# Attention's products with v taken chunk by chunk, and the last 64 keys turned by transpositions

## The chip, the cores and the metric

The kernel runs on one core of a Trainium2 chip. The metric is the device time of one execution in microseconds (us). Engines are named as in the profile: PE is TensorE's matmul queue and PEld its weight loads, DVE is VectorE, ACT is ScalarE, POOL is GpSimd, SP issues most of the transfers.

## The reference

Two parts follow each other: attention over batch 4, 8 heads, 576 positions, head width 64, with a bias that a small network makes of the distance between positions, and a gated feed-forward layer over the 2304 tokens.

```python
scores = q @ k.T / 8 + bias[head]          # 576 x 576 per batch and head
attn = exp(scores - max); attn /= sum(attn)
x = (attn @ v)                              # tokens x 512
h = x @ w_in                                # 512 -> 2048
out = (h * tanh(softplus(h))) @ w_out       # 2048 -> 512
```

The change lies in attention alone, in how `attn @ v` and the transpositions ahead of it are cut up.

## The kernel before, in words

Attention goes over 16 pairs `i`: a pair is one batch and two heads, head 0 in partitions 0 to 63 (`TOP`), head 1 in 64 to 127 (`LOW`). The 576 query rows of a pair are cut into chunks: 0 to 3 with 128 rows, 4 with 64. A step `n` is one chunk of one pair; the chunks of a pair come in the order 0, 1, 4, 2, 3, so 80 steps in all (`x = n % 5`, `c` the chunk). Below, "step x=2" is the third step of a pair.

For its own chunk a step does: `scores(n)` on PE (L226: two heads at once in two halves of the array, three passes of 2 x 288 keys; the first three pairs are in plain float32), `add_bias(n)` on DVE (L243: two instructions, one per head, that take the scores out of PSUM, add the bias and find the row maximum), and `exps(n)` on ACT (L258). The scores have two PSUM buffers per step's two heads in such a way that the scores of a step can begin only when `add_bias` of the step before has emptied them.

A product with v needs the weights with keys on partitions. `transposes(n)` turns chunk n's rows for keys 0 to 511 of both heads by 16 PE transpositions (L296), into two PSUM banks, which ACT copies to the tile `main` (L305, two copies of 128 x 512). The last 64 keys of both heads lie side by side in 128 columns of `pt`; `ends(n)` turns them by two ordinary float32 matmuls against the identity (L321), each of which PE runs as two passes, into a third bank, and ACT copies the result into `tail` (L322). Chunk 4 has its end among the transpositions.

`pv_duo(i, grp, k)` is the product with v: group 0 is chunks 0 and 1 (256 query columns, one `main0`), group 1 is chunks 4, 2, 3 (320 columns). For each of five key blocks k it does one matmul per head (L335, for the last block L339), again two passes each; the two heads stand in two column halves of the array and run side by side. After the fifth block DVE copies the result out of PSUM (L342) and SP stores it to `x_d`. The `products` table in `step` spreads these blocks: two at x=4, two at x=0, one at x=1, three at x=2, two at x=3.

The order on every engine is the order of the calls in `step(n)` (the schedule is manual): scores and bias of n, transpositions of chunk n-2, exponentials of n, reciprocals of the pair before (at x=0), loads ahead, one piece of the conversion of float64 weights (`split`, mostly DVE, L125 to L132; on ACT at x=2), products, and at x=1 and x=4 an extra `ends`. Steps 0 to 2 run inside the stage that makes the bias; steps 3 and 4 have an order of their own. Four more steps, NS to NS+3, finish the last chunks among the first units of the feed-forward layer (`hidden`, L623).

Of the kernel before, what the change touches and what calls it, by code (L numbers as in the profile page):

```python
# [7 lines left out]
F32 = mybir.dt.float32  # L8
# [7 lines left out]
B, H, S, D, C = 4, 8, 576, 64, 32  # L16
# [3 lines left out]
P = 128  # L20
# [25 lines left out]
def kernel(ctx: ExitStack, tc, qk, v, wb, w2, w_in, w_out, psia, psi4, rinv, eye, out):  # L46
# [225 lines left out]
    def turned(i, grp):  # L272
        if (i, grp) not in pt_t:
            w = 256 if grp == 0 else 320
            main = ptp.tile([P, 2, 4, w], F32, name=f"main{grp}")
            tail = ptp.tile([P, 256 if grp == 0 else 384], F32, name=f"tail{grp}")[:, :w]
            pt_t[i, grp] = (main, tail)
        return pt_t[i, grp]

    def place(c):  # L280
        return (0, c * P) if c < 2 else (1, 64 + (c - 2) * P)

    def transposes(n, shared=False):
        i, c = steps[n]
        pt, m = live[n]
        main, tail = turned(i, 0 if c < 2 else 1)
        top, low = (t_ps.tile([P, 512], F32, name="tp") for _ in range(2))
# [9 lines left out]
        inline = c in (2, 3) or (c < 2 and i == 0)  # L297
        if inline:
            copy_end = ends(n)
        if c < 4:  # L300
            off = place(c)[1]
            for g, tp in enumerate((top, low)):
                q0 = off + 64 * g
                copy = dve.tensor_copy if shared and g else act.copy
                copy(main[:, :, :, q0:q0 + 64], tp.rearrange("p (h k q) -> p h k q", h=2, k=4))  # L305
            if inline:
                copy_end()
        else:
            for h, tp in enumerate((top, low)):
                act.copy(main[:, h, :, 0:64], tp[:, :256].rearrange("p (k q) -> p k q", k=4))  # L310
                act.copy(tail[(TOP, LOW)[h], 0:64], tp[(LOW, TOP)[h], 256:320])

    def ends(n):

        i, c = steps[n]
        pt, m = live[n]
        grp, off = place(c)
        tail = turned(i, grp)[1]
        end = t_ps.tile([P, 512], F32, name="tp")
        for h in range(2):  # L320
            pe.matmul(end[h * 64:h * 64 + 64, 0:P], pt[:, 512 + 64 * h:576 + 64 * h], ident, start=True, stop=True)  # L321
        return lambda: act.copy(tail[:, off:off + P], end[:, 0:P])  # L322

    def pv_duo(i, grp, k):
        hp, b = divmod(i, B)
        main, tail = pt_t[i, grp]
        vt = v_t[i]
        w = 256 if grp == 0 else 320
        if k == 0:
            o_t[0] = o_ps.tile([P, 512], F32, name="o")  # L330
        o = o_t[0]
        kw = dict(skip_group_check=True)
        if k < 4:
            for h in range(2):
                pe.matmul(o[h * 64:h * 64 + 64, :w], vt[:, h, k, :], main[:, h, k, :],  # L335
                          start=(k == 0), stop=False, **kw)
            return
        for h in range(2):
            pe.matmul(o[h * 64:h * 64 + 64, :w], vt[:, h, 4, :], tail, start=False, stop=True, **kw)  # L339
        del pt_t[i, grp]  # L340
        x = xs.tile([P, 320], F32, name="x")
        dve.tensor_copy(x[:, :w], o[:, :w])  # L342
        if grp == 0:
            sp.dma_start(out=x_d[b][:, hp, 0:256], in_=x[:, :256])
        else:
# [67 lines left out]
    def step(n):  # L413
        i, x = divmod(n, 5)

        def begin():
            if n < NS:
                scores(n)
                add_bias(n)

        def turn():
            if 0 <= n - LAG < NS:
                transposes(n - LAG)
            if x == 4 and i:
                ends(n - 3)()

        def end():
            if 0 <= n - 1 < NS and (n - 1) % 5 == 4:
                reciprocals((n - 1) // 5)
            if n < NS:  # L430
                ahead(n)
                split(n)

        def products():
            todo = {4: (i, 0, (0, 1)), 0: (i - 1, 0, (2, 3) if i < NPAIR else (2, 3, 4)), 1: (i - 1, 0, (4,) if i < NPAIR else ()), 2: (i - 1, 1, (0, 1, 2)),
                    3: (i - 1, 1, (3, 4))}.get(x, (-1, 0, ()))
            j, grp, ks = todo
            if 0 <= j < NPAIR and (j, grp) != (0, 0):
                for k in ks:
                    pv_duo(j, grp, k)  # L440

        if n in (3, 4):
            scores(n)
            if n == 3:
                transposes(0, True)
            add_bias(n)
            exps(n, 0)
            if n == 3:
                transposes(1, True)
            exps(n, 1)  # L450
            if n == 3:
                transposes(2)
            else:
                for k in range(5):
                    pv_duo(0, 0, k)
            end()
            return
        begin()
        turn()
        if n < NS:  # L460
            exps(n, 0)
            exps(n, 1)
        end()
        products()
        if x == 1 and n < NS:
            ends(n - 1)()
# [105 lines left out]
    ptp = lsbuf("ptp", 1)  # L572
# [5 lines left out]
    t_ps = lpsum("t_ps", 3)  # L578
# [72 lines left out]
    step(NS + 3)  # L651
# [247 lines left out]
```

## Time and profile before

| | us |
|---|---|
| median of 3 runs | 667.78 (667.48 to 668.13) |
| the profiled execution's own time | 669.82 |
| its span, from the first to the last instruction | 667.8 |
| mean granted TensorE clock over the span | 0.994 |

PE is busy for 96% of the span, PEld for 75%, DVE for 68%, ACT for 62%, POOL for 23%. These are means over stages with different limits: the stage that makes the bias reaches to about 60 us, attention to about 296 us, the feed-forward layer to the end. A busy PE in the profile is not PE at its peak, since the ends of matmuls are modelled and overlap; how often PE starts a pass says more than how long it counts as busy.

### The profile page before, as it was taken

The page shows a single profiled execution, that of the slowest core. Times are in us where ns is not written, and L with a number is a line of the kernel's source. Part 1 is how long each engine was busy: PE and PEld are TensorE (multiplying, and loading weights), DVE is VectorE, ACT ScalarE, POOL GpSimd, SP SyncE. Part 2 cuts the span into 40 slices and gives each one's busy share as a digit, 9 for nine tenths or more (in the row PEclk, how much of TensorE's full clock was granted, in tenths as well). Part 3 has the DMA queues.
Part 4 walks back from the last instruction along what each step waited for, and adds up shares of the span by engine and source line. Part 5 has one row for each costly group of instructions (what it writes and reads, how often), then busy time and mean ns, then how long its engine had stood idle before and what let it go on. Part 6 is the DMA issues. An engine that isn't in the chain of part 4 may idle for free.

```text
span 667.8 us, 13803 instructions
## 1 busy us (share of the span) xinstructions
PE 644.1 (96%) x5300; PEld 499.4 (75%) x5300; DVE 450.8 (68%) x822; ACT 412.0 (62%) x871; POOL 150.7 (23%) x142
## 2 busy tenths in 40 slices
PE   6868999999999999999999999999999999999997
PEld 3214667777777777778888998888888888888886
DVE  7995777778888786721433455334699877888874
ACT  6995799989999889862433343343574444454441
POOL 0000133333222231701102120112243321133330
PEclk9997999999999999999999999999999999999999
DMA  4998486677667858106448786733764544433300
GB/s 134 307 313 266 146 253 208 219 224 241 217 219 229 263 167 258 44 19 194 152 153 258 253 220 194 217 124 122 225 190 126 158 151 149 142 117 117 114 32 33
DMA packets 101058, 119.66 MB, mean 179 GB/s; under 512 B 15616, under 2 KB 77568, under 8 KB 100992
## 3 DMA queue, kind: packets, MB, share of 16 engines
q1 hardware_dynamic: 98688, 110.59, 52.5%
q0 software_dynamic: 1872, 8.09, 3.9%
q8 instruction: 42, 0.69, 0.4%
q14 instruction: 24, 0.20, 0.1%
q10 hardware_dynamic: 432, 0.09, 0.1%
HBM read 79.47 MB, written 39.28 MB: 178 GB/s over the span
## 4 chain that ended last, share of the span: by engine, by line
PE 82%; DMA 4%; ACT 3%; DVE 2%; issue 2%; SPq 0%; POOL 0%; DVEq 0%; ACTq 0%
PE h L623 30%; PE s L226 10%; PE o L335 9%; PE y L745 8%; PE h L745 8%; PE tp L296 5%; PE y L746 4%; PE h L746 4%; PE tp L321 3%; PE o L339 2%; DMA x_d<-x 1%; ACT pt L258 1%; DMA xa<-r_d 1%; ACT main L305 1%; DMA xraw<-x_d 1%
## 5 line engine op out<-in xcount | busy, mean ns | idle before, releaser
L258 ACT ACTIVATE pt<-pt,m 128x576 f32<-128x576 f32 x144 | 112.3, 790 | 2.3 <-DVE m L243 2.3
L243 DVE CUSTOM_DVE_ANT_0 pt<-s,bias 128x576 f32<-128x576 f32 (+1 forms) x112 | 81.5, 754 | 34.0 <-PE s L226 31.8
L635 ACT ACTIVATE g<-h 128x512 f32<-128x512 f32 x72 | 42.8, 599 | 73.1 <-PE h L623 61.4
L305 ACT COPY main<-tp 128x512 f32<-128x512 f32 x126 | 68.1, 598 | 25.0 <-PE tp L296 23.5
L335 PE MATMUL o<-main,vt 128*64 128x320 f32 (+1 forms) x512 | 75.9, 420 | 0.0
L177 POOL TENSOR_TENSOR qklo<-rawqk,qkhi 128x304 fp32r<-128x304 f32 x52 | 43.7, 865 | 122.5 <-DMA rawqk<-in_qk_dram 122.5
L639 POOL TENSOR_TENSOR g<-g 128x256 f32<-128x256 f32 (+1 forms) x40 | 33.4, 837 | 159.5 <-ACT g L635 150.5
L623 PE MATMUL h<-xa,lc 128*128 128x512 f32 (+1 forms) x288 | 55.5, 354 | 0.0
L296 PEld LDWEIGHTS tp<-ident,pt 64*128 64x128 f32 x1184 | 51.2, 139 | 4.9 <-ACT main L305 2.4
L296 PE MATMUL tp<-ident,pt 64*128 64x64 f32 x1184 | 52.6, 223 | 2.0 <-ACT main L305 1.9
L623 PEld LDWEIGHTS h<-xa,lc 128*128 128x128 f32 x288 | 47.6, 189 | 7.5
L722 DVE TENSOR_TENSOR gslot<-quarters,gslot 128x1024 fp32r<-128x1024 f32 x28 | 47.0, 1704 | 7.9 <-ACT gslot L721 7.9
L721 ACT CAST gslot<-w 128x1024 fp32r<-128x1024 f32 x30 | 31.5, 1051 | 32.0 <-DVE w L718 19.0
L554 PE MATMUL bps<-ht,w2t 128*32 128x512 f32 (+17 forms) x352 | 35.3, 510 | 16.3 <-ACT bt L536 7.8
L722 DVE TENSOR_TENSOR gslot<-w,gslot 128x1024 fp32r<-128x1024 f32 x30 | 41.1, 1384 | 13.6 <-ACT gslot L721 13.6
L226 PE MATMUL s<-qkhi 64*128 64x288 f32 x260 | 49.3, 343 | 0.1
L721 ACT CAST gslot<-quarters 128x1024 fp32r<-128x1024 f32 x28 | 29.5, 1052 | 31.3 <-DVE quarters L718 19.8
L226 PEld LDWEIGHTS s<-qkhi 64*128 64x128 f32 x260 | 28.1, 184 | 25.9 <-DVE m L243 11.4
L335 PEld LDWEIGHTS o<-main,vt 128*64 128x64 f32 x512 | 33.4, 139 | 17.0 <-issue 2.3
L524 DVE TENSOR_SCALAR ht<-at,bb 128x576 f32<-128x576 f32 (+17 forms) x123 | 44.1, 440 | 0.0
L226 PE MATMUL s<-qklo,qkhi 64*128 64x288 f32 x260 | 42.0, 296 | 0.1
L226 PE MATMUL s<-qkhi,qklo 64*128 64x288 f32 x260 | 41.2, 293 | 0.4 <-POOL qklo L177 0.4
(157 smaller groups left out, 1482.6 us busy)
## 6 DMA issues: line engine op xcount, KB each, us to landing
g_d<-g SPq DMA_DIRECT2D x32, 512.0 KB
bias_d<-bt SPq DMA_DIRECT2D x36, 295.5 KB
w<-in_w_in_dram SPq DMA_DIRECT2D x16, 512.0 KB
w<-in_w_out_dram SPq DMA_DIRECT2D x16, 512.0 KB
quarters<-g_d SPq DMA_DIRECT2D x16, 512.0 KB
qkhi<-in_qk_dram POOLq DMA_DIRECT2D x13, 608.0 KB, 4.9
rawqk<-in_qk_dram SPq DMA_DIRECT2D x13, 608.0 KB
w<-g_d SPq DMA_DIRECT2D x15, 512.0 KB
```

What stands on the lines that cost most here:

```text
L226: pe.matmul(s[:, j, :SH], q[rows, c * P:(c + 1) * P], k[rows, KO + j * SH:KO + (j + 1) * SH], start=(t == 0), stop=(t == len(terms) - 1))
L243: dve.tensor_tensor_reduce(out=halves(pt[rows, sl]), in0=s[rows, :, :SH], in1=halves(bt[rows, sl]), scale=-0.125, scalar=BIG, op0=ALU.add, ...
L258: act.activation(ps, ps, AF.Exp, bias=m[:, u:u + 1], scale=-1.0, accum_out=sums[i][:, k:k + 1])
L296: pe.transpose(tp[:, k * 64:k * 64 + 64], pt[rows, c0:c0 + P], ident[rows, rows])
L305: copy(main[:, :, :, q0:q0 + 64], tp.rearrange("p (h k q) -> p h k q", h=2, k=4))
L335: pe.matmul(o[h * 64:h * 64 + 64, :w], vt[:, h, k, :], main[:, h, k, :], start=(k == 0), stop=False, **kw)
L524: dve.tensor_scalar(ht[:, :n], at[:, :n], bb[:, k:k + 1], 0.0, op0=ALU.add, op1=ALU.max)
L623: pe.matmul(h[:, u * n:(u + 1) * n], w_at(f, d)[t], x[:, d, :n], start=(k == 0), stop=(k == 11))
L721: act.copy(hi, src)
L722: dve.tensor_tensor(lo, src, hi.bitcast(F32), op=ALU.subtract)
L745: pe.matmul(o, hi[:, f], wc[m][:, f], start=(f == 0 and m in (0, 1, 3)), stop=False, **kw)
L746: pe.matmul(o[:, 0:256], lo[:, f], wc[m][:, f, 0:256], start=False, stop=(f == 7), **kw)
```

## The change

Every chunk now has its own product. `products(n)` takes all five key blocks of one chunk, 128 columns (64 for chunk 4), into that chunk's columns of the result's bank; the bank is still copied out after chunk 1 and after chunk 3. It is called for chunk n-3 at the end of step n. `main` holds one chunk and has two buffers, and so has `tail`.

`ends(n)` is no longer two matmuls but two transpositions (one per half of the partitions) of the same 128 columns, and its result is copied by DVE in place of ACT. It is called for chunk n-1 as the last PE work of step n, right ahead of the next step's scores. All transpositions share one PSUM tile of three banks, taken in turn by a counter.

The piece of weight conversion moves to the end of the step, and is left out at x=0 from pair 5 on, where the reciprocals are. It is still done on ACT where a conversion begins at x=2. Step 3 turns chunks 0 and 1 and no longer chunk 2; step 4 takes products of chunk 0 and 1 and turns chunk 2. The last of the four closing steps goes away.

```diff
-    def turned(i, grp):
...
     def place(c):
-        return (0, c * P) if c < 2 else (1, 64 + (c - 2) * P)
+        return (0, c * P) if c < 2 else (1, 0 if c == 4 else 64 + (c - 2) * P)
+    tail_t, x_t, n_tp = {}, {}, [0]
+    def banks_of(k):
+        n_tp[0] += k
+        return [(n_tp[0] - k + j) % 3 for j in range(k)]
+    def ends(n):
+        i, c = steps[n]
+        tail_t[n] = tail = ptp.tile([P, P], F32, name="tail")
+        if c == 4:
+            return
+        pt = live[n][0]
+        t, l = sorted(banks_of(2))
+        for rows, bank in ((TOP, t), (LOW, l)):
+            pe.transpose(tp_t[:, bank, 0:64], pt[rows, 512:640], ident[rows, rows])
+        dve.tensor_copy(tail.rearrange("p (g q) -> p g q", g=2), tp_t[:, t:l + 1:l - t, 0:64])
...
-    def ends(n):
-        end = t_ps.tile([P, 512], F32, name="tp")
-        for h in range(2):
-            pe.matmul(end[h * 64:h * 64 + 64, 0:P], pt[:, 512 + 64 * h:576 + 64 * h], ident, start=True, stop=True)
-        return lambda: act.copy(tail[:, off:off + P], end[:, 0:P])
-    def pv_duo(i, grp, k):
...
+    def products(n):
+        main, tail, vt = pt_t.pop(n), tail_t.pop(n), v_t[i]
+        w = P if c < 4 else 64
+        grp, off = place(c)
+        if c in (0, 4):
             o_t[0] = o_ps.tile([P, 512], F32, name="o")
+        for k in range(5):
             for h in range(2):
+                pe.matmul(o[h * 64:h * 64 + 64, off:off + w], vt[:, h, k, :], main[:, h, k, :w] if k < 4 else tail[:, :w],
+                          start=(k == 0), stop=(k == 4), skip_group_check=True)
+        if c == 1:
+            dve.tensor_copy(x[:, :256], o[:, :256])
+        elif c == 3:
+            dve.tensor_copy(x, o[:, :320])
...
     def step(n):
+        if n < NS:
             scores(n)
+        if n == 3:
+            ends(0)
+            transposes(0, True)
+        if n < NS:
             add_bias(n)
+        if n == 4:
+            products(0)
+        if 4 <= n < NS + LAG:
+            transposes(n - LAG)
+        if n < NS:
             exps(n, 0)
             if n == 3:
+                ends(1)
                 transposes(1, True)
             exps(n, 1)
+            ahead(n)
+        if n >= 4:
+            products(n - LAG - 1)
+        if n <= NS:
+            ends(n - 1)
+        if n and x == 0 and n <= NS:
+            reciprocals(i - 1)
+        if n < NS and (x or i < 5):
+            split(n)
...
-    ptp = lsbuf("ptp", 1)
+    ptp = lsbuf("ptp", 2)
-    t_ps = lpsum("t_ps", 3)
+    tp_t = lpsum("t_ps", 1).tile([P, 3, 512], F32, name="tp")
...
-    step(NS + 3)
```

## Rows read from the trace of the kernel before

**Rows 1.** The page: busy time by engine, and TensorE's granted clock in 40 slices.

```profile
PE 644.1 (96%) x5300; PEld 499.4 (75%) x5300; DVE 450.8 (68%) x822; ACT 412.0 (62%) x871; POOL 150.7 (23%) x142
...
PEclk9997999999999999999999999999999999999999
```

**Rows 2.** Windows: busy us (and instructions) of PE, PEld, DVE, ACT, POOL; clock; DMA.

```profile
96.50:278.53 182.03, 180.95 (x2440) 132.78 (x2438) 141.62 (x378) 166.52 (x441) 56.29 (x67) 1.00 0.67 213
209.53:223.53 14.00, 14.00 (x193) 10.36 (x191) 10.28 (x30) 13.03 (x35) 3.92 (x5) 1.00 0.65 211
59.60:66.50 6.90, 6.04 (x34) 3.67 (x36) 2.16 (x7) 4.47 (x14) 0.00 (x0) 0.51 0.75 227
81.64:96.50 14.86, 14.86 (x172) 10.23 (x170) 11.69 (x31) 13.64 (x37) 6.83 (x8) 1.00 0.81 263
278.53:296.06 17.53, 17.53 (x144) 12.13 (x142) 3.31 (x10) 11.33 (x26) 5.39 (x4) 1.00 0.06 19
```

**Rows 3.** Timeline of PE in pair 11, 212.4 to 223.6: start, us, instruction, count.

```profile
212.42 0.40 PE L226 MATMUL s<-qkhi 64*128 64x288 f32 x2
...
215.03 0.40 PE L226 MATMUL s<-qkhi 64*128 64x288 f32 x2
...
215.79 0.30 PE L226 MATMUL s<-qkhi,qklo 64*128 64x288 f32 x2
215.93 0.65 PE L296 MATMUL tp<-ident,pt 64*128 64x64 f32 x16
216.51 1.83 PE L335 MATMUL o<-main,vt 128*64 128x320 f32 x12
218.28 0.40 PE L226 MATMUL s<-qkhi 64*128 64x288 f32 x2
...
220.99 0.40 PE L226 MATMUL s<-qkhi 64*128 64x288 f32 x2
...
221.90 0.47 PE L296 MATMUL tp<-ident,pt 64*128 64x64 f32 x10
222.29 0.44 PE L321 MATMUL tp<-ident,pt 128*64 128x128 f32 x4
222.56 1.03 PE L335 MATMUL o<-main,vt 128*64 128x256 f32 x8
223.53 0.40 PE L226 MATMUL s<-qkhi 64*128 64x288 f32 x1
```

**Rows 4.** Timeline of DVE in the step whose scores begin at 212.42.

```profile
213.52 0.76 DVE L243 CUSTOM_DVE_ANT_0 pt<-s,xa 128x576 f32<-128x576 f32 x1
...
214.20 0.75 DVE L243 CUSTOM_DVE_ANT_0 pt<-s,xa 128x576 f32<-128x576 f32 x1
214.88 0.08 DVE L243 DVE_READ_ACCUMULATOR2_ANT m<- 128x1 f32 x1
```

**Rows 5.** Timeline of PE, 214.25 to 214.30: one end's second passes, then a product.

```profile
214.07 0.28 PE L321 MATMUL tp<-ident,pt 128*64 128x128 f32 x2
214.18 0.39 PE L339 MATMUL o<-tail,vt 128*64 128x256 f32 x2
```

**Rows 6.** Weight loads (PEld) by line and form, 96.50 to 278.53: busy us, mean ns | idle.

```profile
L335 PEld LDWEIGHTS o<-main,vt 128*64 128x64 f32 x408 | 25.9, 136 | 12.0
```

**Rows 7.** The same view for ACT, 96 to 279.

```profile
L322 ACT COPY tail<-tp 128x128 f32<-128x128 f32 x52 | 14.6, 281 | 0.3
```

**Rows 8.** The same view for DVE, 96.50 to 278.53.

```profile
L132 DVE SCALAR_TENSOR_TENSOR w<-w,w 128x512 uint32<-128x512 uint32 x14 | 11.5, 818 | 0.1
...
L342 DVE COPY x<-o 128x320 f32<-128x320 f32 x12 | 5.8, 480 | 0.3 <-PE o L339 0.3
L342 DVE COPY x<-o 128x256 f32<-128x256 f32 x13 | 5.4, 419 | 0.0
```

**Rows 9.** Timeline of DVE, 190 to 194.5: one piece of weight conversion.

```profile
192.60 1.32 DVE L132 SCALAR_TENSOR_TENSOR w<-w,w 128x512 uint32<-128x512 uint32 x1
```

**Rows 10.** Timeline of PE at step 4, 54.8 to 67.2.

```profile
63.21 3.53 PE L335 MATMUL o<-main,vt 128*64 128x256 f32 x16
```

More of the change, by code (lines that the diff above doesn't have):

```diff
@@ L270, in reciprocals @@
             sp.dma_start(out=r_d[b][hp][:, 32 * g:32 * g + 32], in_=rt[32 * g:32 * g + 9])
-    def turned(i, grp):
[L273 to L278, printed above, removed]
-    def place(c):
-        return (0, c * P) if c < 2 else (1, 64 + (c - 2) * P)
+    def place(c):
+        return (0, c * P) if c < 2 else (1, 0 if c == 4 else 64 + (c - 2) * P)
[13 more added lines that the diff above has]
+        dve.tensor_copy(tail.rearrange("p (g q) -> p g q", g=2), tp_t[:, t:l + 1:l - t, 0:64])
     def transposes(n, shared=False):
         i, c = steps[n]
-        pt, m = live[n]
-        main, tail = turned(i, 0 if c < 2 else 1)
-        top, low = (t_ps.tile([P, 512], F32, name="tp") for _ in range(2))
+        pt = live[n][0]
+        main = ptp.tile([P, 2, 4, P], F32, name="main")
+        pt_t[n] = main
+        top, low = (tp_t[:, bank] for bank in banks_of(2))
         if c < 4:
@@ L296, in transposes @@
                 pe.transpose(tp[:, k * 64:k * 64 + 64], pt[rows, c0:c0 + P], ident[rows, rows])
-        inline = c in (2, 3) or (c < 2 and i == 0)
-        if inline:
-            copy_end = ends(n)
         if c < 4:
-            off = place(c)[1]
             for g, tp in enumerate((top, low)):
-                q0 = off + 64 * g
                 copy = dve.tensor_copy if shared and g else act.copy
-                copy(main[:, :, :, q0:q0 + 64], tp.rearrange("p (h k q) -> p h k q", h=2, k=4))
-            if inline:
-                copy_end()
+                copy(main[:, :, :, 64 * g:64 * g + 64], tp.rearrange("p (h k q) -> p h k q", h=2, k=4))
         else:
@@ L414, in step @@
         i, x = divmod(n, 5)
[L416 to L442, printed above, removed]
+        if n < NS:
             scores(n)
-            if n == 3:
-                transposes(0, True)
+        if n == 3:
+            ends(0)
+            transposes(0, True)
+        if n < NS:
             add_bias(n)
+        if n == 4:
[3 more added lines that the diff above has]
+        if n < NS:
             exps(n, 0)
             if n == 3:
+                ends(1)
                 transposes(1, True)
             exps(n, 1)
[L451 to L466, printed above, removed]
+            ahead(n)
[7 more added lines that the diff above has]
+            split(n)
     bc = bsbuf("bc")
```

24 lines of the change are left out of this document (4 added, 20 removed).

## The prediction, made before the changed kernel ran

> **What bounds the kernel now.** I read the page first: PE is busy for 644.1 of 667.8 us and its clock is at full level but for two short stretches [rows 1]. Then the windows by stage: from the fourth pair on (96.50 to 278.53, 13 pairs) PE is busy for 180.95 of 182.03 us at clock 1.00, ACT for 166.52, DVE for 141.62 [rows 2]; the feed-forward layer behind it has PE busy all the time too, so what attention saves should arrive at the end. Last the timeline of one pair, to see whether PE is busy because it has work or because its passes are stretched by waits. Pair 11 takes 14.00 us [rows 2]; its steps begin at 209.53, 212.42, 215.03, 218.28, 220.99 and the next at 223.53, so they last 2.89, 2.61, 3.25, 2.71 and 2.54 us [rows 2, 3].
>
> Four of the five are PE's own work laid end to end. Step x=2: the scores' first to last pass takes 0.76 (215.03 to 215.79), transpositions start 0.14 later, the product 0.58 after that (16 transpositions against 10 take 0.58 against 0.39, so 0.062 per pair of them, seven gaps, and 0.15 for changing from half rows to half columns), and twelve passes of 320 columns with the change back take 1.77: together 3.25, the whole step. Step x=4 likewise: 0.91 to the transpositions, 0.39 for ten of them, 0.27 for the end, 0.97 for two key blocks of 256 and the change: 2.54 [rows 3]. Step x=1 is different. Its scores start at 212.42, DVE takes them up 1.10 later at 213.52, the second half starts at 214.20, the maximum is read out by 214.96, and the next scores start at 215.03 [rows 3, 4]. That loop (scores, DVE, scores) is a floor of 2.61 us under any step, because the scores have no further buffer. So PE sums bound four steps and the loop one.
>
> **The change part by part.** *Ends.* One end costs PE 0.27: its first pass 0.16, its second 0.11, seen as 214.07 to 214.18 [rows 3, 5]. Four per pair make 1.08 us. They become one pair of transpositions each: the gap between pairs of transpositions is 0.062 and a refill 0.05, so I take 0.11; below it is bounded by 0.06, above by the 0.27 that it replaces. But they now stand alone between product and scores, where the change of 0.10 is due anyway. When scores follow an end without a wait, their own refill is spared: the five gaps among their passes take 0.76, the sixth, to the transpositions, 0.14, so the first carries about 0.1 more than the others.
>
> *Products.* The columns stay: 576 per key block and pair. What grows is the number of passes: 20 instructions for each of five chunks where two groups had 20 each, 60 more per pair. Four pairs of passes of 256 columns take 1.03, one pair 0.39 [rows 3, 5], so they are some 0.216 apart; six pairs of 320 take 1.77 with 0.10 for the change and 0.05 for the refill, 0.27 apart [rows 3]. Per column that is the same, so 128 should take 0.11, which [rows 5] shows once, weight loads included. For a chunk of 128 that is 0.16 + 9 x 0.11 = 1.15; for chunk 4, 0.11 + 9 x 0.056 = 0.61. Sum 5.2 per pair; before, 10 x 0.216 + 10 x 0.27 = 4.86 plus about five refills, 5.1. So products cost nothing net, provided weight loads stay hidden; a load lasts 0.136 in its row [rows 6], which is the upper bound for the gap.
>
> *What moves between steps.* This is where I expect the gain: the 1.77 us product of x=2 is split up. By these terms a step is scores 0.90, transpositions 0.58 (0.39 for chunk 4), product 1.15 (0.61), change 0.10, end 0.11. Steps x=1 and x=2 come to 2.84 each, x=3 (no end, chunk 4 has none) to 2.73, x=4 to 2.65; x=0, with chunk 4's product, to 2.30, so the floor of 2.61 holds there. Sum 13.67; two refills spared take 0.2 off; I add 0.1 for a late DVE (below): 13.6 against 14.0. Over 13 pairs, -5.2. The two earlier whole pairs, in plain float32 (14.86 the second, [rows 2]), have longer scores and so a floor of about 2.8: -0.25 each, -0.5.
>
> *The copies.* ACT loses four copies of 0.281 per pair [rows 7], 1.1 of its 13.03 us [rows 2]. It doesn't set the pace by the step sums, so I count no gain, though no ACT wait can then take PE's place. DVE gets them. Two forms of its copy differ by 0.061 for 64 columns (0.480 and 0.419), so 128 take 0.30 by extrapolation; bounds 0.28 (ACT's) and 0.42 [rows 7, 8]. DVE has 10.28 of 14.00 in pair 11 and would have about 11.4 of 13.6. The copy waits for the end, the last thing on PE, and behind it in DVE's queue stand the reciprocals (x=0) or the piece of conversion, then the next bias step. In a step of 2.84: DVE is free at 2.55, the copy runs from about 3.0 to 3.25 (at x=4 and x=2 the result's copy goes first, 3.34), a piece of conversion, 0.82 for the mean of the longest kind [rows 8], brings it to 4.07 to 4.16, and the next scores are ready at 2.84 + 1.10 = 3.94. Late by some 0.2 at most, which the next step's slack over the floor (0.23) takes up. Leaving the conversion out at x=0 keeps that true beside the reciprocals. Single pieces last 1.32 [rows 9], half a microsecond more than that mean, hence the 0.1.
>
> *Banks.* Ends and transpositions take four banks per step out of three. A transposition finds the end's bank freed by DVE: due 0.9 after the scores start, freed about 0.45 after. An end finds the top bank freed by ACT's first copy, about 0.5 ahead. No wait by these numbers; if it missed, up to 0.3 per step.
>
> *Start.* Step 4 ran at clock 0.51 [rows 2], its 16 passes of a product took 3.53 [rows 10]. Now transposing chunk 2 falls into it too, and ACT's exponentials of step 4 stand behind the copies of that; on the other hand later steps find products done. I take +0.5; bounds -1.5 (full clock sooner) and +2 (one more ACT round).
>
> *Close.* From the last scores to the fourth unit of the feed-forward layer is 17.53 us [rows 2]. By the terms above attention's part of it is 2.54 for step 79, 2.25 (transpositions, end, three blocks of 256, change), 0.95 (transpositions, end, change) and 2.85 (five blocks of 320): 8.6. After the change it is 2.65, then 1.5 (transpositions, chunk 4's product, end, change), 1.85 (transpositions, a product, change) and 1.3 (a product): 7.3 to 7.5 with a change more, so -1.2. In the last pair DVE also makes the first block of tokens (L391, four instructions, by the nearest two-operand row 0.76 each [rows 4], about as much as a step's slack and the left-out piece together), and conversions now reach to step 79 where they ended at 68: +0.8. SP's stores move up with the copies by a step or so; nobody waits for them here.
>
> Sum: -5.2 - 0.5 + 0.5 - 1.2 + 0.8 = -5.6. Against the profiled execution (span 667.8, own time 669.8) that is a span of 662.2 and an own time of 664.2; the median of the runs shown is 667.78, so the forecast is 662.2.
>
> **The rivals.** *A: more than that.* If the sums of 2.84 are too high by the spared refills everywhere, all steps sit near the floor, 5 x 2.61 = 13.05; with 13.2 the gain is 10 and more, 656. ACT's relief speaks for it, the term 0.10 of each change against it.
>
> *B: it is eaten up.* A DVE that is late by 0.08 per step beyond its slack costs 0.4 a pair, which is the gain: 666 to 668. For it: ACT and DVE would both be busy for about 85% of a shorter pair and work strictly in order. Against: the slack of 0.2 in most steps.
>
> *C: slower, DVE becomes the bound.* The copy of an end holds up DVE until PE's last instruction of the step. Where the conversion behind it then takes the 1.32 of [rows 9] the bias step is 0.6 late, 0.4 after the slack. It decides from a lateness of about 0.3 in every step: 14.4 a pair, +0.4 x 15 = +6, 673; with waits for banks on top (the 0.3 above, if a wait on one bank covers the tile) the same size again. For it: DVE's copies at x=2 and x=4. Against: such a piece is one of four in a conversion.
>
> *D: slower, weight loads come into the open.* At 0.136 per pair of passes, 36 passes of 128 lose 0.94 a pair; chunk 4's loss stays under the floor's slack but for 0.3: 14.85, +13, 680. Against: the 0.11 in [rows 5], and transpositions with weights twice as wide, 0.062 apart [rows 3]. The Trainium skill, "TensorE: Matmul & The Clock Gate", section "Back-to-back issue gap", gives some 81 ns per load and multiply at 128 columns in a sustained stream. By it two column halves would take 0.16 per pair of passes, an estimate that would make this rival worse (some 1.9 a pair); the trace's 0.11 contradicts it for this form, though one gap is not a stream.
>
> **How the numbers follow.** Forecast (658 to 666) 0.48; A 0.12; B 0.17; C with its banks 0.18; D 0.05. Of B, 0.05 is still faster by over 0.2% (1.3 us, about what a measurement of this kernel can tell from no change), 0.10 within, 0.02 slower; of C 0.03 stays within. Faster 0.65, same 0.13, slower 0.22. The range 656 to 672 leaves out the better part of A and the worse halves of C and D. The likeliest case's own range is 658 to 666.
>
> **What would show it.** Right: step lengths near 2.6, 2.8, 2.8, 2.7, 2.65 in every pair, none at 3.25; passes of a product 0.11 apart; no wait of PE for DVE's tail copy; clock 1.00 through the 13 pairs. Wrong: a DVE bias step that starts more than 0.4 after the last pass of its scores (rival C or B); gaps of 0.13 or more between products (D); a stretch at half clock longer than 6.9 us at step 4, or a closing stretch still at 17.5.

## The result: 0.6% slower, and the profile after

| | before | after |
|---|---|---|
| median | 668.47 us (666.91 to 671.29, 12 runs) | 672.11 us (670.23 to 676.52, 12 runs) |
| profiled execution's own time | 669.82 us | 671.56 us |
| its span | 667.8 us | 669.8 us |

The ratio is 1.0056 (95% interval 1.0035 to 1.0078): slower, where 662.2 us and faster was forecast, and just outside the range (656 to 672). First the page of the profile after, as [rows 1].

```profile
PE 635.8 (95%) x6132; PEld 530.0 (79%) x6132; DVE 473.3 (71%) x888; ACT 406.8 (61%) x805; POOL 151.5 (23%) x142
...
PEclk9988999999999999999999999999999999999999
```

PE has 832 more passes to start and ACT 66 fewer instructions, as the change says; the clock is at full level but for short stretches, as before. The windows of the same stages, as [rows 2] (the first is pairs 3 to 14, the second pair 11, then step 4, pair 2, the last pair up to its fifth scores, and the close):

```profile
97.48:269.97 172.49, 164.56 (x2906) 148.01 (x2907) 145.48 (x398) 152.16 (x364) 50.13 (x61) 1.00 0.68 218
212.69:226.77 14.08, 13.55 (x244) 12.32 (x245) 11.86 (x34) 12.53 (x31) 3.98 (x5) 1.00 0.62 194
60.00:67.28 7.28, 6.42 (x76) 4.99 (x77) 3.09 (x9) 3.43 (x10) 0.00 (x0) 0.77 0.72 225
82.32:97.48 15.16, 14.63 (x225) 12.33 (x226) 12.76 (x35) 12.94 (x32) 5.81 (x8) 1.00 0.75 243
269.97:283.42 13.45, 11.94 (x200) 10.23 (x200) 13.27 (x30) 9.88 (x23) 7.68 (x6) 1.00 0.21 64
283.42:300.76 17.34, 16.80 (x176) 13.24 (x174) 5.21 (x15) 10.86 (x23) 4.36 (x4) 1.00 0.12 40
```

The same twelve pairs took 169.49 before, so a pair grew from 14.12 to 14.37 in the mean, where 13.6 was forecast. PE is no longer busy from end to end: in the first window it idles for 172.49 - 164.56 = 7.9 us. The steps of a pair, read from the starts of its scores, last 2.80, 2.80, 2.80, 2.71 and then something between 2.84 and 3.40 (2.80 and 3.22 to 3.51 change places in pairs 3 and 4, where conversions still go on in all five steps). Only the fifth varies, with a mean of 3.17 over pairs 3 to 14. The timeline of PE across that step and the next (x=4 of pair 10 and x=0 of pair 11) shows both of its parts:

```profile
209.42 0.85 PE L226 MATMUL s<-qkhi 64*128 64x288 f32 x2
...
210.65 0.60 PE L306 MATMUL tp<-ident,pt 64*128 64x64 f32 x10
211.18 1.10 PE L327 MATMUL o<-main,vt 128*64 128x128 f32 x16
212.10 0.39 PE L327 MATMUL o<-tail,vt 128*64 128x128 f32 x4
212.59 0.27 PE L289 MATMUL tp<-ident,pt 64*128 64x64 f32 x2
212.69 0.40 PE L226 MATMUL s<-qkhi 64*128 64x288 f32 x2
...
214.17 0.69 PE L327 MATMUL o<-main,vt 128*64 128x64 f32 x16
214.68 0.29 PE L327 MATMUL o<-tail,vt 128*64 128x64 f32 x4
215.40 0.28 PE L289 MATMUL tp<-ident,pt 64*128 64x64 f32 x2 [0.43 <-ACT main L310]
```

Scores that wait show no idle time, only passes drawn out: at 209.42 the first two take 0.85 and the transpositions come 1.23 behind the start, where they come 0.88 behind it at 212.69 (213.57). Then the end (L289) at x=0 waits 0.43 for ACT. What made the scores of 209.42 wait stands one step earlier on DVE, and beside it on POOL:

```profile
206.75 0.49 DVE L335 COPY x<-o 128x320 f32<-128x320 f32 x1 [0.19 <-PE o L327]
207.15 0.28 DVE L290 COPY tail<-tp 128x128 f32<-128x128 f32 x1
207.47 1.00 DVE L128 TENSOR_SCALAR w<-w 128x512 uint32<-128x512 uint32 x1
208.39 0.75 DVE L243 CUSTOM_DVE_ANT_0 pt<-s,xraw 128x576 f32<-128x576 f32 x1
```

```profile
206.54 3.42 POOL L177 TENSOR_TENSOR qklo<-rawqk,qkhi 128x304 fp32r<-128x304 f32 x4 [8.86 <-DMA rawqk<-in_qk_dram]
```

The result's copy, the copy of the end and the piece of conversion (L128) stand ahead of the bias step. The piece takes 1.00. The scores of this step (x=3) began at 206.71, so the bias step starts 1.68 behind them, against 1.10 in [rows 3, 4]. What it empties is the PSUM that the scores of 209.42 need.

### The profile page after: what moved, and what is told of

The parts are those of the page before. It is cut to its first block, busy times and chain, and to the rows that moved or that the text cites. A ratio compares the mean times of both kernels' runs of the same rounds, so it can differ in the third digit from the quotient of the medians.

```text
span 669.8 us, 15502 instructions
## 1 busy us (share of the span) xinstructions
PE 635.8 (95%) x6132; PEld 530.0 (79%) x6132; DVE 473.3 (71%) x888; ACT 406.8 (61%) x805; POOL 151.5 (23%) x142
## 4 chain that ended last, share of the span: by engine, by line
PE 74%; ACT 7%; DVE 6%; issue 3%; DMA 2%; SPq 0%; ACTq 0%; DVEq 0%
PE h L587 28%; PE s L226 9%; PE y L708 8%; PE h L708 8%; PE o L327 7%; PE tp L306 5%; PE y L709 4%; PE h L709 4%; ACT main L310 3%; PE tp L289 2%; DVE pt L243 2%; ACT main L313 2%; DMA xlo<-r_d 1%; ACT tail L314 1%; DVE w L128 1%
## 5 line engine op out<-in xcount | busy, mean ns | idle before, releaser
L327 PE MATMUL o<-main,vt 128*64 128x128 f32 (+1 forms) x1280 | 81.9, 271 | 0.0
L327 PEld LDWEIGHTS o<-main,vt 128*64 128x64 f32 x1280 | 64.1, 138 | 6.4 <-issue 1.1
L226 PE MATMUL s<-qkhi 64*128 64x288 f32 x260 | 51.1, 337 | 1.6 <-DVE m L243 1.4
L226 PE MATMUL s<-qklo,qkhi 64*128 64x288 f32 x260 | 43.7, 296 | 0.0
L518 PEld LDWEIGHTS bps<-ht,w2t 128*32 128x32 f32 x352 | 11.2, 117 | 39.1 <-ACT bt L500 27.0
```

What stands on the lines that cost most here:

```text
L226: pe.matmul(s[:, j, :SH], q[rows, c * P:(c + 1) * P], k[rows, KO + j * SH:KO + (j + 1) * SH], start=(t == 0), stop=(t == len(terms) - 1))
L327: pe.matmul(o[h * 64:h * 64 + 64, off:off + w], vt[:, h, k, :], main[:, h, k, :w] if k < 4 else tail[:, :w], start=(k == 0), stop=(k == 4) ...
L518: pe.matmul(ps[cg * 32:cg * 32 + 32, a:min(a + 512, n)], w2t, h_t[idx, cg][:, a:min(a + 512, n)], start=True, stop=True)
```

## The experiments

The expectations name four theories. P: the place of the conversion's pieces; the one at the end of x=2 runs beside POOL's subtractions, is drawn out and makes the next bias step late. Q: the products' shorter passes cost more than their columns. R: that DVE, and not ACT, copies the end. B: the end waits for a bank of PSUM. The table gives medians against runs of the kernel before on the same chip, and two marks of the profile: from the first scores of pair 1 to the fourth unit of the feed-forward layer (228.95 before, 233.48 after), which leaves out the start and the last phase, and the mean of pairs 3 to 14 (14.12 and 14.37). Both marks are of one profile each; the two profiles of the change differ by 1.9 and 0.15.

| kernel | median | ratio (95% interval) | pair 1 to fourth unit | pair |
|---|---|---|---|---|
| change again | 673.11 | 1.0046 (1.0025 to 1.0067) | 231.60 | 14.22 |
| split early | 674.67 | 1.0070 (1.0045 to 1.0095) | 234.74 | 14.47 |
| tail on ACT | 703.89 | 1.0514 (1.0483 to 1.0544) | 262.44 | 16.49 |
| last pair | 674.41 | 1.0072 (1.0048 to 1.0096) | 232.96 | 14.39 |
| place | 667.15 | 0.9973 (0.9945 to 1.0000) | 227.35 | 13.97 |
| place again | 670.37 | 1.0003 (0.9978 to 1.0027) | 227.41 | 13.97 |
| own bank | 670.67 | 1.0019 (0.9988 to 1.0049) | 231.96 | 14.29 |
| own bank and place | 670.17 | 1.0004 (0.9978 to 1.0030) | 229.13 | 14.21 |
| before, other end | 668.03 | 0.9978 (0.9949 to 1.0008) | 228.47 | 14.12 |
| two banks and place | 686.28 | 1.0247 (1.0214 to 1.0279) | 245.03 | 15.20 |
| no POOL | 671.03 | 1.0038 (1.0008 to 1.0068) | 228.83 | 14.02 |
| place and last pair | 667.05 | 0.9993 (0.9970 to 1.0016) | 226.90 | 13.96 |

**The change again**, unchanged.

> The changed kernel once more, as the yardstick for the others of this call. In its first trace step x=4 lasts 2.84 to 3.40 us (forecast 2.65) and x=0 2.80 (forecast 2.61), the others 2.80, 2.80, 2.71 as forecast. Theory P (place): the piece of weight conversion that is issued at the end of step x=2 runs beside POOL's subtraction for the next pair, is stretched, makes the bias step of x=3 late and with it the scores of x=4. Theory Q (passes): the 60 more passes per pair and their weight loads are what costs. Theory R (copy): DVE is over its limit since it copies the ends. All: ratio to before 1.004 to 1.008.

Slower again, by 0.5%; x=4 lasts 2.81 to 3.28. Where the piece L128 falls among POOL's subtractions varies between executions: here it lasts 0.43 to 1.03 in pairs 5 to 14, 0.64 to 1.14 in the first profile, and the pairs are 0.15 shorter. The two profiles together show the price of the piece pair by pair. In the first, x=4 lasts 2.25 to 2.27 more than the piece ahead of it in all ten pairs (2.90 behind a piece of 0.64, 3.40 behind one of 1.14). In the second it lasts 2.24 to 2.26 more in eight pairs, and 2.81 behind the two pieces that take 0.43 and 0.45. So a piece costs nothing up to about 0.55 (2.81 less 2.26), and beyond that all that it is longer.

**All pieces ahead of the products.**

```diff
             ahead(n)
+            if x or i < 5:
+                split(n)
         if n >= 4:
             products(n - LAG - 1)
...
-        if n < NS and (x or i < 5):
-            split(n)
```

> Only the place of the conversion piece is changed: it is issued right behind the bias step, ahead of the products' and the end's copies, where DVE waits for PE anyway. P: the bias step of x=3 is on time (under 0.1 late), x=4 falls to 2.7 to 2.85, a pair from 14.37 to 13.9 to 14.0, -4 to -6 us against the changed kernel, ratio to before 0.996 to 1.000. Q: no change, ratio 1.005. R: the work of DVE is the same, so it is late elsewhere by as much; ratio 1.003 to 1.005.

x=4 falls to 2.83 in every pair, and from pair 4 on x=3 rises to 2.94 to 3.56. Two rows of DVE and one of PE say why: the piece still takes 0.99 beside POOL, but now the copy of the end is behind it, and the next transpositions wait for the bank that this copy frees.

```profile
208.63 0.99 DVE L128 TENSOR_SCALAR w<-w 128x512 uint32<-128x512 uint32 x1
...
210.06 0.28 DVE L290 COPY tail<-tp 128x128 f32<-128x128 f32 x1
```

```profile
210.40 0.71 PE L306 MATMUL tp<-ident,pt 64*128 64x64 f32 x16 [0.58 <-DVE tail L290]
```

The gain that P expected (a pair of 13.9 to 14.0) did not come: the bias step is on time, but moving the piece ahead at x=2 only changed who is late.

**The copy of the end on ACT.**

```diff
-        dve.tensor_copy(tail.rearrange("p (g q) -> p g q", g=2), tp_t[:, t:l + 1:l - t, 0:64])
+        act.copy(tail.rearrange("p (g q) -> p g q", g=2), tp_t[:, t:l + 1:l - t, 0:64])
```

> The ends are copied by ACT, as before the change; all else is as in the changed kernel. R: step x=4 falls to 2.65 to 2.75, -5 us or more, ratio 0.998 or less. P: the piece starts only 0.2 earlier and stays stretched, x=4 falls by about 0.2 and ACT is late in return; ratio 1.001 to 1.005. Q: nothing, 1.005.

5% slower, by far the worst. On ACT the copy stands behind both exponentials, and each following transposition waits for it:

```profile
219.84 0.72 PE L306 MATMUL tp<-ident,pt 64*128 64x64 f32 x16 [0.64 <-ACT tail L290]
```

No theory expected this. With the end as the last work of a step, the copy is far worse placed behind ACT's exponentials than on DVE. It does not decide R by itself, since x=0 to x=2 grew to 3.56 to 3.72; the kernel without POOL's subtractions below does, where DVE copies the ends and x=4 is on time.

**The last pair without conversion.**

```diff
-        if n < NS and (x or i < 5):
+        if n < NS and (x or i < 9) and i < 15:
```

> Conversions are left out in the last pair and made up for by pieces at x=0 in pairs 5 to 8. P: the last pair's steps x=1 to x=3 (2.93, 3.59, 4.13 in the changed kernel) fall to about 2.8 to 3.3, -1.5 to -2.5 us there, and pairs 5 to 8 lose 0.2 to 0.4 each at x=1 or x=2; -0.5 to -2 us in all. Q: the last pair stays as it is.

The last pair falls from 13.45 to 12.88, but the pieces that run instead at x=0 of pairs 5 to 8 cost at least as much earlier (those four pairs take 58.1, against 57.1 and 56.1 in the two profiles of the change): no gain in the sum.

**Pieces at every step but x=2.** Behind the bias step at x=0 and x=1, at the step's end at x=1 (a second piece), x=3 and, up to pair 8, x=4; none in the last pair. The conversions are as many in all.

```diff
             ahead(n)
+            if x < 2 and i < 15:
+                split(n)
...
-        if n < NS and (x or i < 5):
+        if n < NS and i < 15 and (x in (1, 3) or x == 4 and i < 9):
             split(n)
```

> The changed kernel with the conversion pieces placed by where DVE has room: behind the bias step at x=0 and x=1, at the step's end at x=1 and x=3 (and x=4 up to pair 8), none at x=2 and none in the last pair. P: with no piece in the reach of POOL's subtraction ahead of a copy, the bias step of x=3 is on time in every pair, x=4 lasts 2.81 everywhere, a pair 13.9 to 14.0; the fourth feed-forward unit begins 4 to 6 us earlier than in the changed kernel (300 there), ratio 0.997 to 1.001. What stays is x=0 at 2.80 and x=4 at 2.81, where the end waits for ACT's last copy. Q and R: no change, a pair at 14.3.

The pairs are now 2.80, 2.80, 2.80, 2.71, 2.81, but for one step of 3.00 each in pairs 3 and 4 and one of 2.93 in pair 7; x=4 is 2.81 to 2.83 in all twelve. The window of pairs 3 to 14 is 4.9 us shorter than in the first profile of the change (3.0 than in the second), and the mark 6.1 (4.2).

```profile
97.28:264.87 167.59, 160.91 (x2906) 145.87 (x2907) 143.57 (x404) 150.90 (x363) 49.13 (x61) 1.00 0.71 225
```

> The kernel with the pieces of the conversion moved away from x = 2, once more, unchanged, to narrow its interval. Theory P (the place of the pieces is the larger part of the miss): ratio 0.995 to 0.999, fourth unit at 294 to 296, a pair 2.80 2.80 2.80 2.71 2.81. If the first result was a chance of the last phase's two speeds: ratio above 1.000, with the fourth unit still ahead of the 296.06 of before.

The marks repeat to 0.1 us, but the medians don't: 0.9973 and 1.0003. Against the kernel before the profile shows 1.5 us less between the marks, 0.2% of the time, and that is what these runs can't tell from none. P is confirmed for the steps; a kernel faster than before is not. Meeting POOL is not enough to cost time: in pair 9 the piece at the end of x=3 lasts 1.16 beside the subtractions, and the steps behind it 2.81 and 2.80, since no copy stands ahead of it and it begins 2.43 into its step.

**POOL's subtractions left out**, the pieces left where the change has them. This separates P's two halves: that a piece is there, and that it is drawn out.

```diff
-        lo = rawp.tile([P, 1280], F32R, name="qklo")
+        lo = rawp.tile([P, 1280], F32R, name="qklo") if i < PLAIN + 2 else qk_t[i - 2][1]
...
-        for c0 in (608, 912, 0, 304):
+        for c0 in (608, 912, 0, 304) if i < PLAIN + 2 else ():
```

> The changed kernel with its pieces of the conversion where the change has them, but from pair 5 on POOL's four subtractions a pair (L177) are left out: the low parts of q and k of pairs 3 and 4 are used again, so the scores of the later pairs are without their right low parts. Theory P in its narrower form (the piece after x = 2 is late because it runs beside POOL's subtractions and is drawn out): the piece at the start of x = 3 takes 0.42 to 0.44 in every pair, the scores of x = 4 0.75 to 0.78, the step x = 4 2.81 in pairs 5 to 14, a pair 13.92 to 13.95; fourth unit at 295 to 296.5, ratio 0.995 to 1.000. Rival O (the order alone: one more operation of 0.42 behind two copies is enough to make the bias late, drawn out or not): x = 4 stays between 2.95 and 3.4, fourth unit at 298 to 301, ratio 1.003 to 1.006.

The same place in the pair, on DVE, in this kernel:

```profile
205.62 0.28 DVE L290 COPY tail<-tp 128x128 f32<-128x128 f32 x1
205.93 0.43 DVE L128 TENSOR_SCALAR w<-w 128x512 uint32<-128x512 uint32 x1
206.28 0.75 DVE L243 CUSTOM_DVE_ANT_0 pt<-s,xraw 128x576 f32<-128x576 f32 x1
```

The piece takes 0.43, and x=4 2.81 or 2.82 in all ten pairs from 5 to 14. The step's shape is the narrower P's: the order alone (rival O) costs nothing, nor does DVE's copying of the ends (R). The groups of this line between 125 and 265 us (busy us, mean ns) in the changed kernel and here:

```profile
L128 DVE TENSOR_SCALAR w<-w 128x512 uint32<-128x512 uint32 x10 | 9.3, 926 | 0.3
```

```profile
L128 DVE TENSOR_SCALAR w<-w 128x512 uint32<-128x512 uint32 x10 | 4.3, 430 | 0.3
```

The copy L290, which reads PSUM, has a mean of 289 ns in both. From pair 1 to the fourth unit it saves 4.65 of 233.48 (2.8 of the second profile's 231.60). The ratio missed its expectation (1.0038; 0.995 to 1.000) and is not told apart from the change's 1.0046 and 1.0056. In its profile the start was 1.1 us later, the last pair, where POOL still works, stayed at 13.49, and the last phase ran at the slower of its two speeds (last section); how much of the median that explains is open.

**The end as one full-row transposition in a bank of its own**, the other two banks for the transpositions.

```diff
-        t, l = sorted(banks_of(2))
-        for rows, bank in ((TOP, t), (LOW, l)):
-            pe.transpose(tp_t[:, bank, 0:64], pt[rows, 512:640], ident[rows, rows])
-        dve.tensor_copy(tail.rearrange("p (g q) -> p g q", g=2), tp_t[:, t:l + 1:l - t, 0:64])
+        pe.transpose(end_t[:, 0:P], pt[:, 512:640], ident)
+        dve.tensor_copy(tail, end_t[:, 0:P])
...
-        top, low = (tp_t[:, bank] for bank in banks_of(2))
+        top, low = (tp_t[:, bank] for bank in range(2))
...
```

> An end is one transposition of all 128 rows into a bank of its own, the other transpositions keep the two others; the conversion pieces are placed as in the changed kernel. Theory B (banks): x=0 falls from 2.80 to 2.61 to 2.70 and x=4, where no piece is stretched, from 2.81 to 2.65 to 2.70, because an end no longer waits for ACT's copies; the stretched pieces still make x=4 up to 3.4. -0.2 to -0.35 a pair, -3 to -4 us, ratio 0.999 to 1.003. If the bank isn't the cause, x=0 stays at 2.80.

PE's wait at x=0 is gone and x=0 falls from 2.80 to 2.48. But x=2 rises to 2.99, since scores come 0.26 behind an end of this form (0.08 to 0.10 behind the changed kernel's, whose end begins at 206.63 and the scores at 206.71, the end at 212.59 and the scores at 212.69). And x=1 rises to 3.21, 0.22 more than x=2: its scores wait for the bias of a step that came so early, and their first passes are drawn out (0.62 against 0.40):

```profile
200.14 0.33 PE L287 MATMUL end<-ident,pt 128*128 128x128 f32 x1
200.40 0.62 PE L226 MATMUL s<-qkhi 64*128 64x288 f32 x2
...
203.35 0.33 PE L287 MATMUL end<-ident,pt 128*128 128x128 f32 x1
203.61 0.40 PE L226 MATMUL s<-qkhi 64*128 64x288 f32 x2
```

x=4, expected at 2.65 to 2.70, stayed at 2.80 where no piece was drawn out. It pays for the dearer end too, so this form cannot show what the wait for the bank costs there.

With the placement as well:

> Own bank and the new places together. B and P both right: steps near 2.65, 2.80, 2.80, 2.71, 2.67, a pair 13.6 to 13.7, which is what the prediction summed up; fourth feed-forward unit at 290 to 293 (296 before the change), ratio 0.991 to 0.996. If only one is right, 13.9 to 14.1 and 0.997 to 1.002. Q: 14.0 or more.

2.48, 3.22, 2.99, 2.73, 2.80: 0.24 a pair longer than with the placement alone, where 13.6 to 13.7 was expected.

**The kernel before with its end as one such transposition**, all else in its place.

```diff
-        for h in range(2):
-            pe.matmul(end[h * 64:h * 64 + 64, 0:P], pt[:, 512 + 64 * h:576 + 64 * h], ident, start=True, stop=True)
+        pe.transpose(end[:, 0:P], pt[:, 512:640], ident)
```

> One part of the change alone, on the kernel before: an end is one transposition in place of two matmuls, still in the third bank and copied by ACT at the old places; products, copies and conversions as before. By the step sums x=0 and x=4 lose up to 0.16 each, x=1 stays at its loop of 2.61: 13.7 to 13.9 a pair, -2 to -5 us, ratio 0.993 to 0.998. If ACT holds the third bank (its wait at x=1 is in the trace of before) or changing between full and half rows costs more, no change, 0.999 to 1.001.

No difference that can be measured; the pair stays at 14.12. An end of this form takes 0.26 (207.11 to the product's 207.37), where the two matmuls took 0.27 [rows 3].

**The end in two banks that no transposition uses**: its own, and free columns of the products' bank, with the placement.

```diff
-        t, l = sorted(banks_of(2))
-        for rows, bank in ((TOP, t), (LOW, l)):
-            pe.transpose(tp_t[:, bank, 0:64], pt[rows, 512:640], ident[rows, rows])
+        for g, rows in enumerate((TOP, LOW)):
+            pe.transpose(oe_t[:, g, 384:448], pt[rows, 512:640], ident[rows, rows])
...
-            o_t[0] = o_ps.tile([P, 512], F32, name="o")
-        o = o_t[0]
+        o = oe_t[:, 0]
...
```

> The places of the conversion's pieces as in the experiment that put none at x = 2, and the chunk's end in two banks that no transposition of the loop uses: one of its own and the free columns of the products' bank; the end keeps its two half-row transpositions and one copy, so that the full-row end's dearer change to the scores does not come in. Theory B (what was left of the miss is the end waiting for ACT's last copy of the step): x = 0 falls from 2.80 to some 2.6 and x = 4 from 2.81 to some 2.65, the others stay at 2.80, 2.80, 2.71; a pair 13.6 instead of 13.92, over 12 pairs some 4 us less: fourth unit at some 291, ratio 0.990 to 0.993. Rival L (a loop through scores, bias, exponentials and the copies of the transpositions has a floor of some 2.8 a step, whatever the end waits for): what x = 0 gives comes back as a wait of the scores of x = 1, as with the full-row end; a pair 13.9 to 14.2, ratio 0.997 to 1.000.

2.31, 3.18, 3.53, 2.74, 3.36: neither theory's pattern. Sharing a bank with the products made the end wait for DVE's copy of the result, at x=2 and x=4:

```profile
252.30 0.28 PE L288 MATMUL oe<-ident,pt 64*128 64x64 f32 x2
252.38 0.76 PE L226 MATMUL s<-qkhi 64*128 64x288 f32 x2
...
259.03 0.28 PE L288 MATMUL oe<-ident,pt 64*128 64x64 f32 x2 [0.69 <-DVE x L332]
```

Undisturbed by that are x=0 and x=1, 5.49 together against 5.60 with the wait and against the 2.61 + 2.84 = 5.45 forecast. So the wait for the bank is worth some 0.1 at x=0, not 0.2: of the 0.49 that x=0 loses, 0.38 comes back at x=1 as a wait of the next scores (rival L). What it is worth at x=4 stays open, at most 0.16 a pair.

**The last pair's multiplication behind the copy of the end**, with the placement.

```diff
         if n and x == 0 and n <= NS:
             reciprocals(i - 1)
+        scaled(n)
...
+    def scaled(n):
         if NS - 5 <= n < NS - 1:
             d = n - (NS - 5)
```

> The places of the conversion's pieces as in the experiment that put none at x = 2, and in the last pair DVE's multiplication of the feed-forward input (L381 of the changed kernel, with POOL's two operations behind it) is issued after the products, the copy of the end and the reciprocals, not ahead of them. Theory P carried to the last pair (an operation of DVE on SBUF is drawn out to some 1.2 to 1.3 beside POOL's, and what is queued behind it is late): the steps x = 2 and x = 3 of the last pair fall from 3.48 and 3.68 to some 3.2 and 3.1, the fourth unit comes 0.6 to 1.2 us earlier than with the pieces alone: at 293.7 to 295, ratio 0.994 to 0.999. Rival (the multiplication is drawn out wherever it stands, and its place gives nothing): the last pair stays at 12.9, fourth unit 294.7 to 295.8.

The last pair falls from 12.88 to 12.10, the close rises from 16.99 to 17.38; the mark gains 0.5, just less than the expected 0.6 to 1.2: x=2 and x=3 take 3.18 and 3.32. Two rows on DVE and two on POOL show the mechanism at its plainest, first in the changed kernel (an instruction of nine columns that takes 0.16 elsewhere), then here:

```profile
273.28 1.22 DVE L265 TENSOR_SCALAR sums<-sums 128x9 f32<-128x9 f32 x1
```

```profile
273.18 1.29 POOL L382 TENSOR_TENSOR xraw<-xraw,xa 128x512 f32<-128x512 f32 x1 [7.71 <-DVE xa L381]
```

```profile
271.60 1.73 DVE L383 TENSOR_TENSOR xa<-xraw,xa 128x512 fp32r<-128x512 f32 x1
```

```profile
271.48 1.29 POOL L385 TENSOR_TENSOR xa<-xraw,xa 128x512 fp32r<-128x512 f32 x1
```

DVE's instruction ends at 274.50 where POOL's ends at 274.47, and at 273.33, 0.56 after POOL's 272.77, about its own length of 0.66. In these rows the two don't share: DVE's instruction, which begins second, waits for POOL's to end.

## Why the prediction was wrong

Term by term, from the two profiles (us):

| term | forecast | measured |
|---|---|---|
| pairs 3 to 14 (12/13 of -5.2) | -4.8 | +3.0 (172.49 - 169.49) |
| plain pairs 1 and 2 | -0.5 | +0.8 (30.20 - 29.39) |
| start | +0.5 | +0.2 (67.28 - 67.11) |
| last pair to its fifth scores (-0.4 + 0.8) | +0.4 | +0.9 (13.45 - 12.54) |
| close | -1.2 | -0.2 (17.34 - 17.53) |
| to the fourth unit | -5.6 | +4.7 (300.76 - 296.06) |

The span grew by 2.0 only, since the last phase ran faster in the profile of after (last section).

**The step that failed is "The copies":** "Late by some 0.2 at most, which the next step's slack over the floor (0.23) takes up." The order was right (result's copy, copy of the end, piece, bias), and so was the length of a copy: 0.289 against 0.30. But the copies came late: the sum has them done 0.50 into the next step (3.34 less 2.84), and the piece starts 0.76 into it (207.47 less 206.71), since the result's copy begins only when the product ends, as the next scores start. Wrong above all was the piece. It was priced by the mean of its longest kind, though from pair 5 on each of a conversion's four pieces has its fixed place, and at the end of x=2 that is L128, 0.43 when nothing disturbs it; and the mean of 0.82 [rows 8] was read as a property of the instruction, the 1.32 of [rows 9] as a rare mishap. Both are lengths with waits in them: L132 has a mean of 683 ns in the changed kernel, where its place at x=4 is free of POOL's work, and L128 the 926 ns shown above. The transfer that releases POOL's four subtractions lands at x=2 to x=3 in nearly every pair, and it did before: the piece of [rows 9], at 192.60, stands among them on POOL's timeline of that kernel.

```profile
190.15 3.22 POOL L177 TENSOR_TENSOR qklo<-rawqk,qkhi 128x304 fp32r<-128x304 f32 x4 [8.88 <-DMA rawqk<-in_qk_dram]
```

In the kernel before, the piece late in x=3 lasts 0.98 to 1.39 in six of the nine pairs from 5 to 13, whatever its kind. So the trace had the meeting in most pairs, not in one of four. What the change took away is the room: before, such a piece starts 192.60 - 190.14 = 2.46 into its step, directly behind a bias step, with 1.35 left until the next one is due (192.85 + 1.10); even so x=0 is 3.03 to 3.06 behind the four longest (1.30 to 1.39), and 2.89 behind the others but one. Now the piece stands behind both copies with 1.10 - 0.76 = 0.34 left, and 0.55 until x=4 grows by it. So the lateness was not spread as 0.1 a pair but sat in one step: x=4 took 3.17 in the mean against 2.65. Of these 0.52, 0.36 is the lateness (x=4 is 2.81 without it, in both experiments that take it away), 4.3 us in twelve pairs; the other 0.16 belongs to the next point. Rival C had the place, the queue and the 1.32, and its 14.4 a pair and 673 are what came (14.37 and 672.11); it got 0.18, because "such a piece is one of four in a conversion". Its point of decision was wrong all the same (no lateness in every step, but one large one per pair), so that its number came out is luck in part. The sign named for it came: the bias step at 208.39 starts 0.93 after the last passes of its scores (207.46), where more than 0.4 was to show C or B.

The Trainium skill, "SBUF — State Buffer", section "Who interferes with whom", says of DVE and GpSimd that an instruction that needs their shared pair of ports holds it whole, and that the other blocks until it is done. The last pair's rows agree: 1.22 for nine columns. By that rule and POOL's rows in the trace of before, the lateness could have been estimated as up to one whole subtraction, 0.83; the piece was drawn out by up to 0.71 (1.14 against 0.43).

**"Banks" failed too:** "An end finds the top bank freed by ACT's first copy, about 0.5 ahead. No wait by these numbers". Between 97 and 270 us the changed kernel's ends wait for ACT's last copy of the step; the weight loads wait up to four times a pair, PE itself about once (columns: total us, times, longest):

```profile
PEld tp L289 <- ACT main L310: 11.7, 36, 0.9
PE tp L289 <- ACT main L310: 5.8, 13, 0.6
PEld tp L289 <- ACT tail L314: 4.4, 13, 0.4
```

At x=0 of pair 11 the first of ACT's two copies is done at 214.87, about 0.5 ahead of the end at 215.40 as forecast, but the end starts right behind the second, which is done at 215.35:

```profile
214.28 1.08 ACT L310 COPY main<-tp 128x512 f32<-128x512 f32 x2
```

In the program only the last of a step's copies signals, so a wait on the first bank covers them all. It decides x=0 (2.80 against 2.61) and, by these waits, the floor of x=4 (2.81 against 2.65), though no run takes the wait alone away at x=4. The bound named was 0.3 a step; seen is 0.2 and 0.16, of which 0.1 at x=0 would come back with the wait removed.

**Right were** the products (their passes 0.11 apart: sixteen take 1.09 from first start to last end, and the next block starts 0.92 after the first) and so rival D's fall; the steps x=1, x=2, x=3 (2.80, 2.80, 2.71 against 2.84, 2.84, 2.73); the end's 0.11. The start lies within its bounds, but the two profiles of the change (+0.2 and +1.2) can't confirm its +0.5. With the pieces out of POOL's way the pair is 13.92 against the sum of 13.67: the 0.35 of x=0 and x=4 less 0.10 in the other three steps. Of the 0.77 by which a pair missed 13.6, then, 0.40 goes with the place of the pieces (13.97 in that experiment), 0.30 stands between that and the sum of the steps, and 0.07 is what refills less a late DVE took off that sum.

**The floor** of 2.61 "under any step" does not hold step by step: the prediction's own x=4 lasted 2.54, and x=0 came down to 2.48 and 2.31 in the experiments with other banks. Scores that begin early are drawn out, and the time comes back in the next step (3.21 and 3.18), so a sum over steps can't take the floor for x=0 alone.

**The base** was a smaller error: 14.00 is pair 11, the mean of twelve is 14.12, above all since x=0 lasts 2.88 to 3.23 there, pair by pair. Measured from it, the saving in twelve pairs would have been 1.5 us larger than forecast.

**Smaller terms.** In the plain pairs the scores are longer on PE (68.32 - 67.28 = 1.04 to the transpositions against 0.90), so that x=0 to x=2 take 2.97 to 3.00, where the forecast went by a floor of 2.8. Their x=4 takes 3.23 and 3.35. Only the second is the same lateness (a piece of 1.09 beside POOL; 3.00 with the placement). The first is 3.23 with the placement too: there ACT makes a cast of 0.61 ahead of the copies for which the end waits. In the last pair the multiplications were priced at 0.76 each, undisturbed, and the pieces that now reach it went into the same +0.8; L265 took 1.22, L125 1.53 beside POOL. In the close, the first part took 3.30 against 2.65, in part because the last scores were held up by the same lateness (1.16 to the transpositions against 0.90), and the second 2.09 against 1.5, with 0.44 of it the wait for ACT; the last two came as forecast (1.89 and 1.24 against 1.85 and 1.3).

## What to carry to other kernels

When a change puts a DVE instruction on SBUF between PE's last work and what PE needs next, look at what POOL does at that moment, not at the instruction's mean: a group whose single times vary by a factor of two (0.43 to 1.14, 0.68 to 1.39) was one that waits here. Then ask how much room it has until the next thing that is due: here a drawn-out piece directly behind a bias step cost at most 0.2, and behind two copies all that it lasted beyond 0.55. A wait for a buffer goes by the instruction that signals, which can be a later one than the one that frees the buffer. And a sum of PE's work per step holds only until the step gets shorter than the loop through the other engines, so a wait removed in one step partly returns in the next.

## What the runs showed of the hardware, unexpected

**The last phase has two speeds.** The feed-forward layer's second part runs the same instructions at the same granted clock in all kernels, and yet 150 us hold 845 passes of PE in some executions and 861 in others, whatever the kernel: the windows of before, after, and of the placement's second profile (first profile: 862).

```profile
500.00:650.00 150.00, 149.30 (x845) 129.22 (x844) 124.21 (x102) 69.43 (x83) 40.15 (x16) 1.00 0.39 123
```

```profile
500.00:650.00 150.00, 149.26 (x861) 131.29 (x860) 126.68 (x104) 71.41 (x85) 38.36 (x15) 1.00 0.40 127
```

```profile
500.00:650.00 150.00, 149.26 (x845) 129.18 (x844) 124.24 (x103) 69.81 (x83) 39.04 (x16) 1.00 0.39 123
```

It makes about 3 us over that phase: 888 passes of it (its 97th to its 985th) take 156.95 or 156.96 us in eight of the fourteen profiles and 154.00 in the other six, with nothing between. That is nearly as much as the whole effect studied, and is the reason for the marks above. What sets it is open; the medians contain both.

**A full-row pass is dear to leave.** Scores start 0.26 behind one 128 x 128 transposition and 0.08 to 0.10 behind two half-row ones. How much of this is the longer pass itself (128 columns against 64) is not separated.
